# FNet and H3 layers on one core: the order of the queues from a timeline model, with one landing buffer and one work buffer fewer

## The chip, the core and the metric

The kernel runs on one core of one Trainium2 chip. A core has five engines that each work through a queue of their own: TensorE (matmuls; PE in the profile, with its weight loads shown apart as PEld), VectorE (DVE), ScalarE (ACT), GpSimd (POOL) and SyncE (SP, which here only issues transfers). Transfers between the core's memory SBUF and the main memory are issued by SP or ACT and carried by 16 DMA engines. Matmuls write to eight accumulator banks (PSUM). An engine runs its queue strictly in the listed order: an instruction that waits holds up all behind it.

The metric is the time of one execution on the device in microseconds (us). Each kernel was run three times, and one further execution was recorded by the hardware profiler; all durations, waits and clocks come from that record.

## What is computed

Two kinds of layer in turn, twice, on an input of 2048 rows and 576 columns:

```python
def _A_ref(x, dft_seq_re, dft_seq_im, dft_hid_re, dft_hid_im):
    a = jnp.einsum("bsd,ed->bse", x, dft_hid_re)
    b = jnp.einsum("bsd,ed->bse", x, dft_hid_im)
    y = jnp.einsum("ts,bse->bte", dft_seq_re, a) - jnp.einsum("ts,bse->bte", dft_seq_im, b)
    return y

def _B_ref(q, k, v, shift_k, ssm_k, ssm_D):
    ...            # kv = (short causal convolution of k, 4 taps) * v
    ...            # y = causal convolution of kv with ssm_k, length 2048, by FFT
    y = y + kv * ssm_D[None, None, :]
    return q * y

x = A_x
x = x + _A_ref(_layernorm(x), ...)
x = x + _B_ref(_layernorm(x), B_k, B_v, ...)
x = x + _A_ref(_layernorm(x), ...)
x = x + _B_ref(_layernorm(x), B_k, B_v, ...)
```

`_B_ref`'s convolution depends on k, v and the filters alone, and both B layers use the same ones, so its result `y` is computed once. In the kernel this is "the branch". What remains of a B layer is the product of the normed x with `y`.

## The kernel before

Every float32 factor is split into a high and a low part of fewer bits (`split`, line 61: ScalarE copies the high part on line 62, VectorE subtracts on line 63), and each product is three matmuls: high by high, high by low, low by high. All matmuls go through `mm`, so all have line 56 in the profile; they are told apart by what they write.

**Main work, `layer` (line 195).** One FNet layer is 128 steps: 4 row blocks `tb`, each with the real and the imaginary DFT matrix (`g` = 0 and 1), each over 16 chunks `k` of the sequence. A step loads one 128x512 chunk of the matrix (`load_c`: tiles `craw`, three buffers, and its split `csp`, three buffers) and multiplies it with the tile `X[k]` in 14 matmuls of 512 columns into the five banks `s0` to `s4`. Counted over both layers there are 256 steps; steps 0 to 127 are the first layer. After the 16 steps of a group, `evac_u` and `evac_r` bring the five banks to the tiles `u` of that `g` (one buffer each).

**`hidden` (line 170).** With the `u` of both `g`, the DFT along the columns is done for the four `j` of the row block: per `j` two pieces of 27 matmuls of 288 columns into one bank `bk` (three banks in all), against the constants `W`. VectorE adds the residual (line 182), which was landed in a `land` tile, into a `work` tile, and `done0` stores it as `xa` (in the first layer), or `done1` gates it and stores the output (in the second). Eight such pieces of 27 follow each row block; `finish(pending, 1)` spreads them over steps, and `finish(pending, 99)` before the last step of the next `g` = 0 group empties the list, since `evac_u` then writes over the `u` that they read.

**The branch (line 230)** runs beside the first layer, in three stages that hand over through main memory:

- f1: for 16 `j` and two sources (`src` 0 is the product of k's convolution and v, on VectorE, lines 278 to 281; `src` 1 is the filter), a split into a `parts` tile (two buffers), 12 matmuls, four evictions (line 295) into `outp` (three buffers) and two stores to `t_d`. Its constants land through `load_fr` (line 77) into `fc`. The chunks of k and the taps use tiles of the tags `w0` to `w8`, which `load_w` needs later for the constants of `hidden`.
- mid: 64 groups; each lands 288 KB of `t_d` in a `land` tile, splits it to `parts`, multiplies (6 matmuls, two banks), multiplies the two spectra on ScalarE and VectorE (lines 327 to 336, two `work` tiles), splits the product to `yf`, multiplies back (3 matmuls, `mid_inverse`, one bank), evicts (line 347) and stores to `v_d`.
- i2: for 16 `j`, lands `v_d` twice and the constants once, splits, 12 matmuls, two evictions (line 383) and a store to `yb`. Each reads all that mid stored.

**The second layer's x.** `get_x1` (line 431) lands `xa` and `yb`, gates (`gated`, line 393, which takes statistics, a power on GpSimd on line 94, and two VectorE operations, lines 398 and 399), stores `xb`, norms it (`normed`, with a second set of statistics and a second power) and writes the split `X[j]` (`to_x`, line 105: ScalarE on line 107, VectorE on lines 109 and 110). For `j` below 12 it is called from step 113 of the first layer on, for the others within the second layer.

**What sets the order.** The program is written out in one order, by the loops at the end of `fnet_h3_kernel`: line 460 to 467 advance the branch by so many pieces per step, up to fixed step numbers (`F1_END`, `W_END`, `MID_END`, `I2_END`). The framework then schedules it: it knows what each instruction reads and writes, places instructions on their engines' queues with the written order as the priority, holds an instruction back while its data or a free buffer of its tag is missing, chooses the addresses (`auto_bufs=True`) and puts in the semaphores. How many tiles of a tag may be alive at a time is the `bufs=` of the tile: `LAND` for all landings of `land` (x, xa, xb, yb, f1's sources, constants, mid's and i2's inputs, the residuals of `hidden`), `WORK` for `work` (normed and gated x, the residual sums, the convolution of k, mid's products).

Of the kernel before, what the change touches and what calls it, by code (L numbers as in the profile page):

```python
# [34 lines left out]
PREP = 113  # L35
MID_LAG = 2
FC = 3
LAND = 5
WORK = 4
PARTS = 2  # L40
OUTP = 3
CRAW = 3
# [4 lines left out]
def fnet_h3_kernel(ctx: ExitStack, tc: tile.TileContext, x, c_mat, w_re, w_im, k_pad, v, shift_k,  # L47
# [17 lines left out]
    def land(shape=(P, D)):  # L65
        return sb.tile(list(shape), F32, tag="land", bufs=LAND, name="land")

    def work(shape=(P, D)):
        return sb.tile(list(shape), F32, tag="work", bufs=WORK, name="work")

# [481 lines left out]
```

## Time and profile before

| | |
|---|---|
| median of three runs | 1257.85 us (1254.85 to 1259.23) |
| span of the profiled execution, first to last instruction | 1256.2 us |
| mean granted TensorE clock | 0.995 of full speed |
| transfers | 200.46 MB, 160 GB/s over the span |
| busy: VectorE, ScalarE | 724.7 us, 579.5 us |

The profiled execution lies 1.65 us below the median of the runs. Busy times are sums over an engine's instructions; the shares are of the span. They are means over stages that differ: in the first 200 us the DMA engines are busy for 0.83 of the time at 274 GB/s and VectorE for 167 of 200 us, from 750 us on (the second layer without the branch) the same figures are 0.32, 99 GB/s and 164 of 450 us. A row of a group of instructions ends in the idle time that its engine had just before them and in what ended that idle time.

### The profile page before, as it was taken

The page shows a single profiled execution, that of the slowest core. Times are in us where ns is not written, and L with a number is a line of the kernel's source. Part 1 is how long each engine was busy: PE and PEld are TensorE (multiplying, and loading weights), DVE is VectorE, ACT ScalarE, POOL GpSimd, SP SyncE. Part 2 cuts the span into 40 slices and gives each one's busy share as a digit, 9 for nine tenths or more (in the row PEclk, how much of TensorE's full clock was granted, in tenths as well). Part 3 has the DMA queues.
Part 4 walks back from the last instruction along what each step waited for, and adds up shares of the span by engine and source line. Part 5 has one row for each costly group of instructions (what it writes and reads, how often), then busy time and mean ns, then how long its engine had stood idle before and what let it go on. Part 6 is the DMA issues. An engine that isn't in the chain of part 4 may idle for free.

```text
span 1256.2 us, 17885 instructions
## 1 busy us (share of the span) xinstructions
PE 1221.6 (97%) x6464; PEld 1059.2 (84%) x6464; DVE 724.7 (58%) x1404; ACT 579.5 (46%) x1166; POOL 54.5 (4%) x68
## 2 busy tenths in 40 slices
PE   7999999999999999999999899999999999999997
PEld 6778788898889888889887898889888988898887
DVE  7799893858865698853488846243324323333324
ACT  6865565758855698853663414221222113201320
POOL 1100000000000000000012201000000000000001
PEclk9999999999999999999999999999999999999999
DMA  8879876745543455447886545223322422233201
GB/s 301 298 249 302 259 256 225 231 124 166 156 135 120 144 159 171 131 153 265 267 280 214 175 141 172 81 87 100 104 84 69 125 88 77 83 100 115 84 35 58
DMA packets 113131, 200.46 MB, mean 160 GB/s; under 512 B 11665, under 2 KB 36241, under 8 KB 113042
## 3 DMA queue, kind: packets, MB, share of 16 engines
q1 hardware_dynamic: 84114, 166.27, 42.6%
q10 hardware_dynamic: 28928, 33.04, 7.4%
q8 instruction: 51, 0.84, 0.3%
q14 instruction: 38, 0.31, 0.1%
HBM read 152.08 MB, written 47.19 MB: 159 GB/s over the span
## 4 chain that ended last, share of the span: by engine, by line
PE 76%; DMA 9%; DVE 6%; ACT 5%; issue 2%; POOL 1%; SPq 0%; ACTq 0%; POOLq 0%; DVEq 0%
PE s L56 50%; PE bk L56 26%; DMA t<-outp 5%; DMA craw<-in_c_mat 2%; POOL rs L94 1%; DVE bst L88 1%; ACT csp L62 1%; DMA land<-t 1%; ACT outp L295 1%; DVE work L399 1%; DVE x L110 1%; DVE parts L63 0%; DVE csp L63 0%; DVE u L63 0%; DMA land<-vd 0%
## 5 line engine op out<-in xcount | busy, mean ns | idle before, releaser
L56 PE MATMUL s<-csp,x 128*128 128x512 f32 x3584 | 855.7, 391 | 3.4 <-DVE csp L63 2.5
L56 PEld LDWEIGHTS s<-csp,x 128*128 128x128 f32 x3584 | 664.1, 188 | 134.2 <-DVE csp L63 3.4
L62 ACT ACTIVATE csp<-craw 128x512 fp32r<-128x512 f32 x256 | 160.6, 629 | 444.3 <-PE s L56 440.5
L63 DVE TENSOR_TENSOR csp<-craw,csp 128x512 fp32r<-128x512 f32 x256 | 176.3, 689 | 313.9 <-ACT csp L62 312.7
L56 PE MATMUL bk<-w,u 128*128 128x288 f32 x1536 | 217.2, 297 | 3.9 <-DVE u L63 2.7
L56 PEld LDWEIGHTS bk<-w,u 128*128 128x128 f32 x1536 | 210.6, 189 | 9.0 <-DVE u L63 3.1
L56 PE MATMUL bk<-parts,fc 128*128 128x288 f32 x576 | 94.8, 306 | 15.8 <-ACT parts L62 8.1
L56 PEld LDWEIGHTS bk<-parts,fc 128*128 128x128 f32 x576 | 86.4, 193 | 26.3 <-ACT outp L295 11.1
L63 DVE TENSOR_TENSOR parts<-land,parts 128x576 fp32r<-128x576 f32 x112 | 84.7, 757 | 29.2 <-ACT parts L62 25.3
L94 POOL TENSOR_TENSOR rs<-ve,mhalf 128x1 f32<-128x1 f32 x56 | 47.6, 851 | 1161.9 <-DVE ve L92 1129.7
L62 ACT ACTIVATE parts<-land 128x576 fp32r<-128x576 f32 x112 | 76.4, 683 | 13.9 <-DMA land<-vd 7.1
L182 DVE TENSOR_TENSOR work<-land,bk 128x288 f32<-128x288 f32 x64 | 28.8, 452 | 88.1 <-PE bk L56 86.3
L56 PE MATMUL bk<-parts,mc 128*128 128x288 f32 x384 | 67.2, 300 | 1.6 <-ACT parts L62 1.0
L295 ACT ACTIVATE outp<-bk 128x288 f32<-128x288 f32 x128 | 47.6, 405 | 41.6 <-DMA t<-outp 28.4
L56 PEld LDWEIGHTS bk<-parts,mc 128*128 128x128 f32 x384 | 56.7, 189 | 8.1 <-ACT parts L62 2.5
L62 ACT ACTIVATE u<-s 128x512 fp32r<-128x512 f32 x64 | 36.4, 599 | 28.1 <-PE bk L56 17.8
L278 DVE TENSOR_TENSOR work<-kr,wt 128x576 f32<-128x576 f32 x64 | 47.1, 752 | 1.7 <-DMA kr<-in_k_pad 1.4
L63 DVE TENSOR_TENSOR u<-s,u 128x512 fp32r<-128x512 f32 x64 | 42.5, 687 | 7.0 <-ACT u L62 6.9
L56 PE MATMUL bk<-yf,mc 128*128 128x288 f32 x192 | 39.7, 303 | 2.3 <-ACT outp L347 1.7
L56 PEld LDWEIGHTS bk<-yf,mc 128*128 128x128 f32 x192 | 32.4, 189 | 10.6 <-ACT outp L347 2.6
L334 DVE TENSOR_TENSOR work<-bk,work 64x288 f32<-64x288 f32 x64 | 29.4, 459 | 19.1 <-ACT work L330 18.6
L62 ACT ACTIVATE yf<-work 128x288 fp32r<-128x288 f32 x64 | 28.3, 442 | 22.8 <-DVE work L336 20.4
(56 smaller groups left out, 702.6 us busy)
## 6 DMA issues: line engine op xcount, KB each, us to landing
craw<-in_c_mat SPq DMA_DIRECT2D x256, 256.0 KB, 3.1
t<-outp ACTq DMA_DIRECT2D x64, 288.0 KB, 4.3
land<-t SPq DMA_DIRECT2D x64, 288.0 KB, 3.0
land<-in_x SPq DMA_DIRECT2D x32, 288.0 KB, 3.6
vd<-outp ACTq DMA_DIRECT2D x64, 144.0 KB, 3.1
land<-vd SPq DMA_DIRECT2D x32, 288.0 KB, 4.3
land<-yb SPq DMA_DIRECT2D x32, 288.0 KB, 3.1
kr<-in_k_pad SPq DMA_DIRECT2D x10, 576.0 KB, 6.2
```

The lines of the kernel that those rows point to most:

```text
L56: nc.tensor.matmul(ps, lhsT, rhs, start=first, stop=last)
L62: nc.scalar.activation(h, src, AF.Copy)
L63: nc.vector.tensor_tensor(l, src, h.bitcast(F32), OP.subtract)
L88: nc.vector.bn_stats(st[:, i, :], src[:, i * HD:(i + 1) * HD])
L94: nc.gpsimd.tensor_tensor(rs, ve, mhalf, OP.pow)
L110: nc.vector.tensor_tensor(t[:, D + REM:], y[:, :NC * P], h[:, :NC * P], OP.subtract)
L182: nc.vector.tensor_tensor(xa[:, cs], r[:, cs], ps[:, :HD], OP.add)
L278: nc.vector.tensor_tensor(tmp if t else r, kr[j + t], w, OP.mult)
L295: nc.scalar.activation(so[:, c, :], ps[:, :HD], AF.Copy)
L334: nc.vector.tensor_tensor(p2[lo], px[hi, :HD], kk[hi, 1, :], OP.mult)
L399: nc.vector.scalar_tensor_tensor(q, q, rs, xa, op0=OP.mult, op1=OP.add)
```

## The change

`LAND` goes from 5 to 4, `WORK` from 4 to 3, and the framework's scheduler is told to run its timeline model of the machine while it places the instructions: an instruction goes onto its queue at the moment at which the model has its engine free and its inputs and buffers there. Instructions, sizes and the written order stay.

```diff
-LAND = 5
-WORK = 4
+LAND = 4
+WORK = 3
...
-    with tile.TileContext(nc, auto_bufs=True) as tc:
+    with tile.TileContext(nc, auto_bufs=True, schedule_with_timeline_sim=True) as tc:
         fnet_h3_kernel(tc, **args, out=o)
```

## The prediction

> **What bounds the kernel now.** I read the page first (busy shares), then the chain of waits, then the windows by stage for the two kinds of matmul, then the groups by form and the DMA issues, and last the order in which the built kernels list their instructions on each engine.
>
> ```profile
> PE 1221.6 (97%) x6464; PEld 1059.2 (84%) x6464; DVE 724.7 (58%) x1404; ACT 579.5 (46%) x1166; POOL 54.5 (4%) x68
> ```
>
> TensorE is busy 97% of the span, so what is left to win is small. How small, the chain says: in its undisturbed stretches it gives the pace of both matmuls.
>
> ```profile
> 746.83 3.60 PE bk L56 x27
> 750.43 79.36 PE s L56 x350
> ```
>
> 350 matmuls of 512 columns (`s`) in 79.36 us are 0.2267 us each; 27 of 288 columns (`bk`) in 3.60 (the next in 3.55) are 0.1324 each. All 3584 `s` and 2880 `bk` make 812.5 + 381.3 = 1193.8 us. No order can go below that; the span has 62 us more. Where they lie, the windows tell (columns: width; busy and count of these matmuls; granted clock; DMA share; GB/s). First `s`, then `bk`:
>
> ```profile
> 0.00:200.00 200.00, 139.79 (x564) 0.99 0.83 274
> ...
> 650.00:750.00 100.00, 66.24 (x283) 0.98 0.57 185
> 750.00:1200.00 450.00, 367.77 (x1604) 1.00 0.32 99
> ```
>
> ```profile
> 0.00:200.00 200.00, 60.37 (x348) 0.99 0.83 274
> ...
> 650.00:750.00 100.00, 31.45 (x215) 0.98 0.57 185
> 750.00:1200.00 450.00, 90.18 (x652) 1.00 0.32 99
> ```
>
> Width minus counts times paces: 0 to 200 loses 200 - 564 x 0.2267 - 348 x 0.1324 = 26 us, 750 to 1200 loses 0.1, and 650 to 750 (the change of layers) 7.4. By the same sum 200 to 250 loses 3.5, 250 to 500 12, 500 to 650 5, and the end after 1200 6.5. So the second layer can only get worse, and before it some 50 us are lost, 6.6 of them before the first matmul.
>
> **What the change does to the order.** All instructions and their sizes stay; what moves is their place. I counted them in the listed orders. "Step" is one of the 256 C chunks (14 `s` matmuls, 3.17 us).
>
> 1. The branch falls behind. When step 32 is done, 240 of 384 f1 matmuls are listed in the kernel before, 159 in the changed one; by step 48, 384 against 282. By step 96, 360 mid matmuls against 264. By step 112, 156 i2 matmuls against none.
> 2. Three things wait for the branch. The w tiles share tags with `kr` and `wt`, so `load_w` follows f1; `hidden` needs w; `evac_u` at the end of each g = 0 group needs the u tiles that `hidden` reads. So steps 48 and 112 can't go on until f1, respectively the last mid groups and 216 `hidden` matmuls, are through. `get_x1` needs all of i2.
> 3. So three stretches have no `s` work for cover: after step 47, 87 f1 matmuls in a row and then 39 mid and inverse ones; after step 111, seven mid groups; and in steps 128 to 138 each step is listed directly behind the x it needs. Before step 128 the kernel before has 9 of the second layer's 16 x written, the changed one 1.
>
> **What each costs.** The rows:
>
> ```profile
> L295 ACT ACTIVATE outp<-bk 128x288 f32<-128x288 f32 x128 | 47.6, 405 | 41.6 <-DMA t<-outp 28.4 <-PE bk L56 12.1 <-ACT outp L295 0.3
> ...
> L328 ACT ACTIVATE work<-bk 64x288 f32<-64x288 f32 x64 | 25.8, 403 | 0.9
> ```
>
> ```profile
> t<-outp ACTq DMA_DIRECT2D x64, 288.0 KB, 4.3
> land<-t SPq DMA_DIRECT2D x64, 288.0 KB, 3.0
> ...
> vd<-outp ACTq DMA_DIRECT2D x64, 144.0 KB, 3.1
> land<-vd SPq DMA_DIRECT2D x32, 288.0 KB, 4.3
> ```
>
> **A, up to step 47.** Fewer f1 items run here, and 0 to 200 moves 274 GB/s at a DMA share of 0.83, so some of its 26 us should come back. 15.6 of them lie in the first 50 us (132 `s`, 34 `bk`), where x and C must land either way; the other 11 could. Against it, SP now issues 4.6 MB of `kr` and `wt` among the first five x loads (8.7 MB up to the fifth, 3.3 before); 5.4 MB at the 300 GB/s of the page's first slice delay it by 18 us, of which the first steps' own matmuls hide part: a loss up to 12. I take 0, near the middle of -11 and +12. POOL's list is the same as before.
>
> **B, step 47 to 48.** f1: 86 matmuls are 11.4 us. ScalarE needs 29 x 0.405 (L295) + 7 x 0.683 (parts) + 1.3 (fc, mc) = 17.8; the 16 stores and five loads, 5.8 MB, need 19 us at 300 GB/s and 23 at 250. I take 20.5: 9 us of stall (6.5 to 11.5). Then the first mid load must follow the last store: 0.4 + 4.3 + 3.0 + 0.68 (split) less 0.8 of matmuls still to run = 7.6 (5 to 9). SP queues the w loads behind that load, so they are late too. Up to the first `hidden` VectorE has 6 x 0.757 (parts) + 10 x 0.755 (w) + 20 x 0.455 (L333 to L336) + 4 x 0.456 (yf) = 23.0 us, ScalarE 21.2, TensorE 64 x 0.132 = 8.5: 14.5, of which I take 13 (11 to 18), since some loads land during the wait before. Less the 3.5 lost there now: **+26** (19 to 35).
>
> **C, steps 48 to 79.** Mid groups are spread thinner among the steps, so some of the 12 us comes back: **-4** (-8 to +3). Around step 80, six mid groups between `hidden` pieces of 27 (3.57 us each, against 3.1 of ScalarE per group): **+2** (0 to 6).
>
> **D, step 111 to 112.** One mid group is 4 x 0.403 + 0.683 + 0.442 + 0.410 = 3.15 us of ScalarE, and the next group's bank comes free only behind L335. Seven groups are 22 us at the least (28 if evictions and VectorE follow each other, 4.0 each); I take 3.5 each, 24.5, against 8.5 us of matmuls: +16 (13.5 to 19.5). What stands behind the waits there: in ScalarE's queue L347 waits for the inverse matmul, and behind it are the next group's L327 to L330, for which L333 and the next bank wait. Then i2: last eviction 0.4, store 3.1, load 4.3, split 0.68, less 1.1 of cover: +7.4 (6 to 9). The alternating i2 and `hidden` pieces after it, four landings in flight instead of five: +4 (0 to 10). Less today's 5: **+22** (15 to 34).
>
> **E, steps 128 to 143.** One x costs VectorE 0.86 + 0.20 + 0.15 (statistics), 0.81 + 0.82 (L398, L399), 0.91 + 0.20 + 0.15, 0.21, 0.22 + 0.68 (L109, L110) = 5.2 us, with the step's csp 0.69 5.9, against 3.17 of TensorE. The two POOL powers (0.85 each, one pair per x) stand between VectorE instructions that need them; 7.2 with their wait whole. I take 6.5. Ten x: 65 + 3.2 for the last step, against 35.4 of matmuls listed there: +33 (27 to 40). The 135 `hidden` matmuls then cover the next x's; the last four follow too closely (chain from `hidden` to x some 16 us by rows: 0.46, store 2.3, load 3.1, then the x): +6 (0 to 10). Less today's 7.4: **+32** (20 to 43).
>
> **F, the clock.** Long gaps cost twice:
>
> ```profile
> 45.00:50.00 5.00, 1.93 (x11) 0.94 0.83 306
> 50.00:55.00 5.00, 5.00 (x18) 0.72 0.73 244
> ```
>
> 3.1 us idle, and the next 5 us run 18 matmuls at 0.72 where 24 fit at 1.00: 6 x 0.227 = 1.4 us. Four long gaps (two in B, two in D): **+6** (0 to 12). In E a slower matmul hides behind VectorE. The Trainium skill, "TensorE: Matmul & The Clock Gate", section "What's actually happening", says the array's clock falls to half after an idle window of about 3.4 us and is freed after about as long a busy one; the dip after the 3.1 us above agrees. By that rule the sparse mid stretches run at half clock too, and F would be nearer 12.
>
> The end (6.5) and steps 144 to 255 stay: there every matmul's producer is listed over 3 us of matmul work ahead, as before.
>
> **Sum:** 0 + 26 - 4 + 2 + 22 + 32 + 6 = +84 on the profiled 1256.2: 1340. The runs' median is 1.65 above that span, so 1342.
>
> **Rivals.**
> - *Thinner stalls, one price:* each clump takes only what its busiest engine is busy, and A gives its 11 back: the low ends, -11 + 19 - 8 + 0 + 15 + 20 + 0 = +35, 1293. For it: engine rows are hard minima, waits are my reading. Against: one queue feeds the next in turn. Chance 0.17 (up to 1310).
> - *The first stages become free of DMA (not slower):* if the loss up to step 111 is all DMA pressure, thinning the branch gives back 26 - 6.6 + 3.5 + 12 = 35 us, and the clumps' engines run far enough ahead for B and D to add nothing; it decides where E stays under 35: 1258 - 35 + 32 = 1255. For it: the 0.83 share and 28.4 us of waits on stores in L295's row. Against: `parts` has two buffers, so splits can't run ahead by more than two items, and mid needs banks, three in all. Chance 0.04.
> - *Half clock:* the clump matmuls and each restart at half pace, plus the high ends of B, D and E: +110 to +140, 1368 to 1398. For it: the dip shown. Against: in the clumps TensorE isn't the bound. Chance 0.17.
> - *It does nothing:* two fewer buffers and the same order. Excluded by the listed orders, which differ in over half their rows.
>
> The forecast itself, between 1310 and 1368, has 0.62. The low and high ends added up give 1293 and 1403 (+145); the range 1296 to 1390 leaves out about 0.1 on either side. A measurement here tells some 0.3% (4 us) from no change. The second rival's 0.04 is halved between faster and same, as its 1255 lies at the border: faster 0.02, same 0.02, slower 0.96.
>
> **What would show it.** TensorE's busy share falls to about 92%. Its waits go to L295 and parts at step 48 (around 210 to 260 us), to L330, L335, L347 and then parts at step 112 (around 570 to 620), and to x (L107, L109, L110) in steps 128 to 143. By the windows some 30 us are lost at each of the three, and nothing after the last. Wrong would be: less than 10 us lost at step 48 (then B's engines ran ahead), or steps 128 to 138 at 3.2 us each (then the x were ready, and E falls).

## The result, and the profile after

The changed kernel takes 1353.64 us (median, 1351.17 to 1354.97) against 1256.35 us of the kernel before (1254.64 to 1259.23), each over four executions with the profiled one among them: the ratio is 1.0765 (95% interval 1.0742 to 1.0789). It is slower, by 97 us where 84 were forecast and inside the range. The profiled execution has a span of 1349.4 us, 93.2 above the span before, and a mean clock of 0.962. A few executions in the experiments took far longer than all others of their kernel (1497.77 us at a clock of 0.754 is one) and are left out of times and ratios; the one that was profiled of the kernel with the two buffers alone is of that kind, so of that kernel only the time is used.

The busy line of the page: TensorE has the same 6464 matmuls, which now fill 93% of a longer span.

```profile
PE 1253.0 (93%) x6464; PEld 1083.2 (80%) x6464; DVE 730.8 (54%) x1404; ACT 588.9 (44%) x1166; POOL 44.1 (3%) x68
```

The waits of TensorE in the changed kernel (total us, times, longest):

```profile
PE s L56 <- ACT x L107: 31.6, 16, 3.2
PE bk L56 <- ACT parts L62: 26.9, 5, 8.6
PE bk L56 <- ACT yf L62: 13.9, 9, 3.1
PE bk L56 <- ACT outp L295: 9.2, 7, 3.7
PE bk L56 <- ACT work L330: 4.3, 5, 1.1
```

The first row is the second layer's x (20.1 us, from 750 us on) and the first layer's own x at the start (11.5 us, in the first 100); `parts` is the start of each stage, `yf` and L330 are mid groups without cover, L295 is f1's.

Where they lie, the windows tell, first for `s`, then for `bk` (width; busy and count; granted clock; DMA share; GB/s). Before:

```profile
0.00:100.00 100.00, 72.92 (x294) 0.98 0.85 284
550.00:650.00 100.00, 54.06 (x224) 1.00 0.78 260
```

```profile
0.00:100.00 100.00, 20.45 (x100) 0.98 0.85 284
550.00:650.00 100.00, 50.66 (x357) 1.00 0.78 260
```

After:

```profile
0.00:100.00 100.00, 62.02 (x239) 0.91 0.69 227
...
200.00:300.00 100.00, 26.69 (x106) 0.83 0.63 205
...
600.00:750.00 150.00, 59.45 (x242) 0.92 0.59 191
750.00:900.00 150.00, 96.03 (x359) 0.93 0.55 170
```

```profile
0.00:100.00 100.00, 11.06 (x51) 0.91 0.69 227
...
200.00:300.00 100.00, 57.08 (x309) 0.83 0.63 205
...
600.00:750.00 150.00, 81.43 (x491) 0.92 0.59 191
750.00:900.00 150.00, 35.46 (x256) 0.93 0.55 170
```

Width minus counts times the two full paces (0.2267 and 0.1324) is the time lost in a stretch: in the first row after 100 - 239 x 0.2267 - 51 x 0.1324 = 39.1. The table has this sum for the matching stretches of both kernels, and the prediction's terms (half of F, the clock, put to B and half to D). The stretches do not hold the same steps, since the branch lags: 550 us is in step 99 before, 600 us in step 109 after.

| stretch (us before; after) | lost before | lost after | moved | predicted |
|---|---|---|---|---|
| start (0-100; 0-100) | 20.1 | 39.1 | +19.0 | A: 0 for both rows |
| (100-200; 100-200) | 5.8 | 0.4 | -5.4 | |
| around step 48 (200-250; 200-300) | 3.5 | 35.1 | +31.6 | B and F: +29 |
| between (250-550; 300-600) | 14.3 | 6.8 | -7.5 | C and step 80: -2 |
| around step 112 (550-650; 600-750) | 2.0 | 30.1 | +28.1 | D and F: +25 |
| change of layers (650-750; 750-900) | 7.4 | 34.7 | +27.3 | E: +32 |

The moves add up to 93.1 of the span's 93.2. After 900 us nothing is lost (0.5 in 400), as forecast. Four terms are within 6 us, and their misses cancel in part (+2.6 and +3.1 against -5.5 and -4.7). The start is not: nothing was predicted there, and 13.6 us came, about as much as the whole forecast is off.

### The profile page after: what moved, and what is told of

Same layout as the page of the kernel before. It is cut to its first block, busy times and chain, and to the rows that moved or that the text cites. A ratio compares the mean times of both kernels' runs of the same rounds, so it can differ in the third digit from the quotient of the medians.

```text
span 1349.4 us, 17915 instructions
## 1 busy us (share of the span) xinstructions
PE 1253.0 (93%) x6464; PEld 1083.2 (80%) x6464; DVE 730.8 (54%) x1404; ACT 588.9 (44%) x1166; POOL 44.1 (3%) x68
## 4 chain that ended last, share of the span: by engine, by line
PE 81%; ACT 5%; DVE 4%; DMA 3%; issue 2%; POOL 0%; ACTq 0%; SPq 0%; POOLq 0%; DVEq 0%
PE s L56 55%; PE bk L56 26%; DMA t<-outp 1%; DVE bst L88 1%; ACT x L107 1%; ACT outp L295 1%; ACT csp L62 0%; DVE work L399 0%; ACT parts L62 0%; DVE work L398 0%; ACT work L330 0%; ACT work L102 0%; DVE x L110 0%; ACT work L329 0%; DMA land<-in_x 0%
## 5 line engine op out<-in xcount | busy, mean ns | idle before, releaser
L56 PE MATMUL s<-csp,x 128*128 128x512 f32 x3584 | 882.0, 396 | 32.2 <-ACT x L107 31.6
L56 PE MATMUL bk<-w,u 128*128 128x288 f32 x1536 | 222.0, 299 | 1.5 <-ACT work L330 1.2
L56 PE MATMUL bk<-parts,fc 128*128 128x288 f32 x576 | 101.4, 311 | 28.5 <-ACT parts L62 19.0
L56 PEld LDWEIGHTS bk<-parts,fc 128*128 128x128 f32 x576 | 92.1, 200 | 39.4 <-ACT parts L62 20.5
L56 PE MATMUL bk<-parts,mc 128*128 128x288 f32 x384 | 79.2, 325 | 13.6 <-ACT parts L62 7.9
L56 PEld LDWEIGHTS bk<-parts,mc 128*128 128x128 f32 x384 | 67.3, 208 | 24.2 <-ACT parts L62 8.5
L182 DVE TENSOR_TENSOR work<-land,bk 128x288 f32<-128x288 f32 x64 | 28.7, 452 | 97.1 <-PE bk L56 92.4
L94 POOL TENSOR_TENSOR rs<-ve,mhalf 128x1 f32<-128x1 f32 x56 | 38.7, 700 | 1264.8 <-ACT outp L383 671.6
L295 ACT ACTIVATE outp<-bk 128x288 f32<-128x288 f32 x128 | 49.7, 408 | 53.0 <-PE bk L56 43.4
L333 DVE TENSOR_TENSOR work<-bk,work 128x288 f32<-128x288 f32 x64 | 29.2, 457 | 59.8 <-ACT work L328 33.1
L56 PE MATMUL bk<-yf,mc 128*128 128x288 f32 x192 | 46.9, 319 | 13.9 <-ACT yf L62 13.9
L56 PEld LDWEIGHTS bk<-yf,mc 128*128 128x128 f32 x192 | 36.0, 203 | 20.8 <-ACT yf L62 16.8
L62 ACT ACTIVATE yf<-work 128x288 fp32r<-128x288 f32 x64 | 28.4, 443 | 29.3 <-DVE work L336 28.7
```

The source lines that it names most:

```text
L56: nc.tensor.matmul(ps, lhsT, rhs, start=first, stop=last)
L62: nc.scalar.activation(h, src, AF.Copy)
L94: nc.gpsimd.tensor_tensor(rs, ve, mhalf, OP.pow)
L182: nc.vector.tensor_tensor(xa[:, cs], r[:, cs], ps[:, :HD], OP.add)
L295: nc.scalar.activation(so[:, c, :], ps[:, :HD], AF.Copy)
L333: nc.vector.tensor_tensor(p1, px[:, :HD], kk[:, 0, :], OP.mult)
```

## The experiments

All are read against the kernel before on the same chip (1255 to 1257 us in the medians); ratios carry their 95% interval. "Lost" is the sum just shown.

### The two buffers alone

```diff
-LAND = 5
-WORK = 4
+LAND = 4
+WORK = 3
```

> The kernel before with LAND 4 and WORK 3 alone, scheduled as before. Theory (the new order costs the time; the two buffers only matter through it): 1250 to 1264 us, within 0.6% of before, and no long wait at steps 47, 111 or 128. Rival (one landing and one work buffer fewer starve the branch, which then lags): 1285 us or more, with waits for land or work tiles in f1 and mid.

1265.70 us, ratio 1.0078 (1.0052 to 1.0104): +10 us, 2 more than my theory allowed and far from the rival. I then took the landing buffer alone (`LAND = 4`):

> The kernel before with LAND 4 alone, WORK 4 and the schedule as before. LAND 4 with WORK 3 had cost 9.8 us. Theory (the landing buffer costs it: SP's queue waits for a buffer, with the loads of C and x behind it, in the first 100 us): 1261 to 1266, the loss in the first 100 us. Rival (the work buffer costs it, through normed x and the convolution of k): within 3 us of before.

1264.4 us, ratio 1.0063 (1.0040 to 1.0086): +8, so most of the 10 is the landing buffer's, and the intervals leave it open whether the work buffer costs anything. 24.0 us are lost in its first 100 us against 20.1: 3.9 of the 5.3 us by which its span is above the one before. No other stretch moves by more than 1 us (6.6 against 5.8 in the second 100, 20.7 against 19.8 from 200 to 650, 8.3 against 7.4 at the change of layers). The other way (`LAND = 6`):

> The kernel before with LAND 6, all else as it was. LAND 4 cost 7.9 us. Theory (SP's queue still waits for landing buffers with five, with C and x behind it): 1249 to 1254, some us won in the first 100. Rival (five are enough, or a sixth only moves bytes to a busier moment): 1254 to 1259.

1259.32 us, ratio 1.0028 (1.0015 to 1.0042): 3.5 us slower, at the upper end of the rival's range. The theory falls: five are enough in the old schedule.

### k's chunks among the first x

In the listed order of the changed kernel SP issues k's chunks and the taps early: in its trace eight of these transfers (576 KB each) go out ahead of the fifth x, where the kernel before has none. By hand in the kernel before, at the head of f1:

```diff
+        load_w4()
+        for i in range(6):
+            load_k(i)
+        loaded[0] = 6
         todo = [(j, 1) for j in range(K_FIRST)] + [(j, 0) for j in range(K_FIRST)]
```

> The kernel before with k's chunks for all the branch's early items and the taps landed among the first x loads instead of one by one ahead of the item that needs them. Theory (those 4.6 MB delay the first x and constants; this is the loss of the changed kernel's first 100 us): +10 to +20 us, 1267 to 1277, the loss within the first 100 us. Rival (the first 100 us are lost to how the landings of x are ordered against each other with four buffers, not to k): under +5, at most 1262.

1264.29 us, ratio 1.0063 (1.0041 to 1.0085): +8, between the two theories. 26.5 us are lost in the first 100 us, 6.4 more than before, so the place is right and the size was too high. But the hand-made order is only half a copy: in its trace four of the eight transfers go out ahead of the fifth x and the others up to 40 us, so 6.4 is not the whole price that they have in the changed kernel. With both buffers cut as well:

> LAND 4, WORK 3 and k's early chunks and taps landed among the first x loads, otherwise the order before. Theory (the changed kernel's loss in its first 100 us is these two parts together, 10 and 9 us): 1270 to 1279, with the loss in the first 100 us. Rival (both are the same waiting of SP's queue and overlap): 1264 to 1269.

1271.94 us, ratio 1.0119 (1.0092 to 1.0146): the time is nearly the sum of the parts, but its first 100 us lose 27.7, 7.6 more than before, where the landing buffer (3.9) and k (6.4) alone add up to 10.3. So the time lies in the theory's range, and in the start the two overlap, as the rival had it. The copy is weaker still here: two of the eight transfers go out ahead of the fifth x.

### f1's last quarter without cover

LAND 4 and WORK 3, f1 thinned over the first 45 steps, and the rest of it and the loads of w behind step 46:

```diff
+        if n == 46:
+            want = 32
+        elif n < 46:
+            want = K_FIRST + 22 * n // 46
...
-        if F1_END < n <= W_END:
-            for _ in range(-(-9 // (W_END - F1_END))):
+        if n == 46:
+            for _ in range(9):
```

> The order before, LAND 4 and WORK 3, with f1 thinned so that its last quarter, the loads of w and nothing of mid stand between steps 46 and 48. To be read against the kernel with these buffers alone. Theory (f1's evictions, stores and loads set the pace of a clump without cover): f1's clump takes 18 to 22 us against 10 of matmuls, +15 to +25 us in all, less what thinning gives back earlier (up to 5). Rival (the engines run ahead of the clump and it goes at matmul pace): under +5.

1287.83 us, ratio 1.0248 (1.0225 to 1.0271) to the kernel before and 1.0248 / 1.0078 = 1.017, or +21 us, to the buffers alone. Around step 48 (200 to 300 us) 18.3 us are lost against 3.9. The clump's last 75 matmuls, 9.9 us of work, go from 227.36 to 249.68 in the timeline, 12.4 us more. Meanwhile ScalarE's evictions (L295) wait 8.0 us for stores to free their tile, and TensorE waits for the evictions. So f1's evictions and stores set its pace; the rival falls. But the clump is only 12.4 of the 21, so that the time lies in the theory's range is in part luck. What I had not expected: the first 100 us lose 32.0, though the second give back 3.8. This pacing puts seven items into the first 16 steps where the kernel before has four, so f1 competes with the first x, as I read it.

### The last mid groups without cover

The buffers as before; mid's groups spread to step 110, the rest of them behind it, and i2 in the eight steps that follow:

```diff
-        elif n <= MID_END:
-            want = 32 + 64 * (n - F1_END) // (MID_END - F1_END)
+        elif n < 110:
+            want = 32 + 53 * (n - F1_END) // 70
+        elif n == 110:
+            want = 96
         else:
-            want = min(113, 96 + 17 * (n - MID_END) // (I2_END - MID_END))
+            want = min(113, 96 + 17 * (n - 110) // 8)
...
-        if n > W_END:
+        if W_END < n < 96 or n > 110:
```

> The order and buffers before, with mid thinned so that nine mid groups stand in a row behind step 111, hidden's 189 matmuls behind them, and i2 after those in eight steps. Theory (ScalarE sets the pace of a mid group without cover, 3.5 to 3.8 us against 1.2 of matmuls): 18 to 24 us in the clump, 3 to 6 more at the change of layers, since x follows i2 (5 of 16 x written by then): +20 to +30, 1275 to 1286. Rival (mid's engines run ahead through the three banks): under +6.

1278.53 us, ratio 1.0181 (1.0135 to 1.0226): +23, in the theory's range. The timeline shows the groups at an even pace (start; length; idle time before and its releaser):

```profile
591.29 0.61 PE L56 MATMUL bk<-yf,mc 128*128 128x288 f32 x1 [1.01 <-ACT yf L62]
...
595.02 0.61 PE L56 MATMUL bk<-yf,mc 128*128 128x288 f32 x1 [1.01 <-ACT yf L62]
```

3.73 us per group, of which 9 x 0.1324 = 1.2 are matmuls, and each waits for `yf`. That ScalarE sets this pace is only part of it. Two groups in a row, each from one inverse matmul to the next (width; busy and count of TensorE, its weight loads, VectorE, ScalarE, GpSimd; clock; DMA share; GB/s):

```profile
576.92:580.12 3.20, 1.99 (x10) 1.31 (x10) 2.90 (x7) 2.94 (x8) 0.00 (x0) 0.98 0.58 179
580.12:583.84 3.72, 2.71 (x9) 2.22 (x10) 2.95 (x7) 2.92 (x8) 0.00 (x0) 0.50 0.46 130
```

ScalarE and VectorE do the same work in both. At full clock ScalarE is busy for nearly the whole group; at half clock a group takes 0.5 us longer, and ScalarE's eviction L347 waits 0.7 us for the inverse matmul instead of 0.2. TensorE is a link of the chain there, though it is far from busy with matmuls of full pace.

### The second layer's x, late

`PREP = 200` in the kernel before: `get_x1` is called in the second layer alone.

> The kernel before with the second layer's x written inside that layer alone (1 of 16 is written before step 128, as in the changed kernel; 9 before). Theory (the x chain sets the pace of steps 128 to 138): each of those steps waits 2 to 3 us for x and takes 5 to 6 us, +20 to +30 us, 1278 to 1288. Rival (x written on time is hidden behind the matmuls, and the loss after step 128 in the changed kernel comes from elsewhere, such as i2 being late): under +6, at most 1263.

1271.14 us, ratio 1.0112 (1.0088 to 1.0137): +14, half of what I expected. The steps without cover have the expected pace:

```profile
772.92 3.53 PE L56 MATMUL s<-csp,x 128*128 128x512 f32 x14 [1.29 <-ACT x L107]
778.62 3.72 PE L56 MATMUL s<-csp,x 128*128 128x512 f32 x14 [2.17 <-ACT x L107]
```

That is 5.7 us from step to step (5.9 to the next one). But there are fewer such steps: in this kernel's list hidden's last matmuls stand between steps 128 and 135, 13 to 27 to a step, and cover the wait. In the changed kernel 135 of them stand in a row behind step 138. So I held them back, calling `finish` in the second layer only from step 136 on:

```diff
-        finish(pending, 1)
+        if n == 8:
+            finish(pending, 99)
+        elif n > 8:
+            finish(pending, 1)
```

> The kernel with the second layer's x in that layer alone (1271 us), and in it hidden's pieces held back in the written order until step 136, so that 81 of those 216 matmuls stand behind step 138. Theory (in the changed kernel the late x cost 27 us and not 14 because hidden's matmuls were spent elsewhere than between the steps that wait for x): 81 x 0.132 = 10.7 us less cover, +5 to +11 on the kernel with late x, 1276 to 1283. Rival (the position of hidden's matmuls does not matter, since x is late by the same amount): 1268 to 1274.

1277.85 us, ratio 1.0171 (1.0148 to 1.0193): +7 on the kernel with late x alone, and the time lost at the change of layers (650 to 800 us) goes from 21.7 to 28.5. That is 21 more than the 7.4 before, against 27.3 in the changed kernel. The rival falls: the same late x costs more where its cover stands behind it.

### All parts together

k's early chunks, LAND 4 and WORK 3, f1's and mid's clumps and the late x in one kernel with the old schedule:

> All four parts of the changed order built by hand into the old schedule, with LAND 4 and WORK 3: k's early chunks among the first x, f1's last quarter behind step 46, the last mid groups behind step 111, the second layer's x in that layer alone. Theory (the parts make the difference and add): 1255 + 18 + 21 + 23 + 14 = 1331, with 1318 to 1350. Rival (the loss is in the fine order of the timeline schedule, which this kernel does not copy): under 1305.

1335.72 us, ratio 1.0635 (1.0607 to 1.0664): +80 of the changed kernel's +97, with the expected sum missed by 5. The first 100 us lose 34.7 (39.1 in the changed kernel), and 600 to 900, both late stretches, 61.8 (64.8). Around step 48 it is 18.6 against 35.1; there this kernel has f1's clump, but not the 39 mid and inverse matmuls behind it. So in the two late stretches the lag of the branch and of x, written by hand, costs about what it costs under the timeline model. The start agrees by another way: thinning f1 by hand loses 32.0 us there even without k's chunks, and puts 93 of the branch's matmuls ahead of step 16, where the changed kernel has 51.

### The timeline order with the old buffers

```diff
-CRAW = 3
-CSP = 3
+CRAW = 2
+CSP = 2
```

and LAND 5, WORK 4 in the changed kernel.

> The changed kernel's timeline schedule with LAND 5 and WORK 4 as before; so that this fits, CRAW and CSP go from 3 to 2. Theory (the timeline order makes the loss; the two buffers about 10 us of it): 1335 to 1365, with the same three losses at steps 48, 112 and 128. Rival (the buffers starve the branch under the timeline): under 1300.

1333.16 us, ratio 1.0619 (1.0590 to 1.0648), 2 us below the theory's range. The order makes most of the loss: 29.7 us are lost around step 48, 27.3 around 112, 30.0 at the change of layers. Giving the buffers back takes away 20 us, not 10, and half of it, 39.1 - 28.7 = 10.4, in the first 100 us. (CRAW and CSP are smaller here, so 20 is the net of both edits.)

SP's waits in the first 100 us, for the landing buffer of the next x (line 419), which is free once ScalarE has normed an earlier one (lines 411 and 102). First the changed kernel, then this one:

```profile
SPq L419 <- ACT work L411: 13.8, 3, 7.1
SPq L419 <- ACT work L102: 12.3, 6, 5.7
```

```profile
SPq L419 <- ACT work L102: 5.4, 3, 3.8
...
SPq L419 <- ACT work L411: 3.5, 3, 1.7
```

26.1 us against 8.9. In all SP waits about as long in both (72.4 and 69.2 us, all rows summed); in the second it waits for C's buffers instead (28.5 us on line 125, against 1.9). While SP waits for a place for x, nothing behind it is issued, the next chunks of C among it: from 50 to 100 us the changed kernel moves 175 GB/s at a DMA share of 0.57, this one 226 at 0.72.

### One more eviction buffer

`OUTP = 4` in the kernel before, since f1's evictions are what TensorE waits for there:

> The kernel before with OUTP 4 in place of 3, all else as it was. TensorE waits 7.7 us for f1's evictions (L295) there, and those wait for stores to free their buffer. Theory (a fourth buffer takes part of that away): 1248 to 1253. Rival (stores of f1 are held up by the DMA engines in the first 200 us, and another buffer only moves the wait): 1254 to 1259.

1254.95 us, ratio 0.9996 (0.9984 to 1.0009): the same time, as the rival had it. None of the kernels beats the one before.

## Why the prediction held, and which term failed

**A, the start: the term that was mis-sized.** The prediction took 0, between -11 and +12. Measured: +19.0 in the first 100 us, -5.4 in the second, +13.6 together. Cut by steps, its two parts stand apart. Steps 16 to 47 lose 1.5 us (96.8 to 232.8 us) against 11.2 (76.8 to 268.6), so the gain from the thinned f1 came nearly in full. All before step 16 loses 39.0 us against 18.2: 20.8 more, where the delay of the first steps was priced at 12 at most. The fifth x goes out at 22.5 us, in the kernel before at 10.4. The working had counted the bytes that k puts ahead of x, but gave the buffer that is missing there no price: it named four landings in flight only in D.

What the runs put in its place, in the first 100 us: the timeline order with the old buffers loses 28.7, that is +8.6, and the step to four and three buffers under it +10.4 more (net, since CRAW and CSP were smaller in the first). In the old order one landing buffer is +3.9, k's early chunks, half copied, +6.4. How the +8.6 splits between k's bytes and the order of x on SP, and the +10.4 between LAND and WORK, stays open: no run changes one of these alone.

**B, step 48: right** (+29 with its clock, +31.6 measured). Lines of the changed kernel's timeline:

```profile
234.15 1.75 PE L56 MATMUL bk<-parts,fc 128*128 128x288 f32 x12
...
240.91 5.83 PE L56 MATMUL bk<-parts,fc 128*128 128x288 f32 x24 [3.71 <-ACT outp L295]
...
261.73 2.12 PE L56 MATMUL bk<-parts,mc 128*128 128x288 f32 x6 [5.79 <-ACT parts L62]
...
283.52 4.93 PE L56 MATMUL bk<-w,u 128*128 128x288 f32 x24 [0.68 <-ACT work L330]
```

f1's clump took from 234.15 to the idle time before 261.73, that is to 255.94: 21.8 us (20.5 predicted); the start of mid waited 5.79 (7.6); mid and w took 283.52 - 261.73 = 21.8 (8.5 + 14.5 = 23, of which 21.5 were entered). VectorE is busy for 19.6 us of these and ScalarE for 19.3, so the bound was the one named. The working set 64 matmuls against it, where its own list and the trace have 39 (5.2 us): the stall was 16.6, with 13 entered.

**C: right in sign.** -7.5 against -2, inside its bounds.

**D, step 112: right** (+25 with its clock, +28.1 measured).

```profile
624.61 0.61 PE L56 MATMUL bk<-yf,mc 128*128 128x288 f32 x1 [1.02 <-ACT yf L62]
...
628.40 0.61 PE L56 MATMUL bk<-yf,mc 128*128 128x288 f32 x1 [1.02 <-ACT yf L62]
...
635.54 4.73 PE L56 MATMUL bk<-w,u 128*128 128x288 f32 x24 [0.55 <-ACT work L330]
...
662.50 3.48 PE L56 MATMUL bk<-parts,fc 128*128 128x288 f32 x12 [4.91 <-ACT parts L62]
```

A group takes 3.79 us (3.5 predicted), and its wait is for `yf`, which the prediction did not name. The clock is 0.50 from 620.81 to 632.21 us, and the kernel with mid's last groups without cover shows what that does: 3.20 us a group at full clock, 3.72 at half. So the prediction's 3.5 came near with one link of the chain left out. The start of i2 waited 4.91 (7.4).

**E, steps 128 to 143: right in mechanism, 5 us too high** (+32, +27.3 measured). An x was priced at 6.5 us; it takes 5.7 to 5.8:

```profile
788.29 5.08 PE L56 MATMUL s<-csp,x 128*128 128x512 f32 x14 [2.30 <-ACT x L107]
...
799.90 3.47 PE L56 MATMUL s<-csp,x 128*128 128x512 f32 x14 [2.29 <-ACT x L107]
```

The window over five such steps of the changed kernel (width; busy and count of TensorE, its weight loads, VectorE, ScalarE, GpSimd; clock; DMA share; GB/s):

```profile
788.29:816.98 28.69, 20.50 (x70) 15.05 (x70) 25.05 (x71) 10.69 (x15) 5.32 (x10) 0.88 0.70 210
```

28.69 / 5 = 5.74 us per step, with VectorE busy for 25.05 of 28.69: it sets the pace. The 5.9 us of listed VectorE work were no lower bound, though: VectorE is busy for 5.01 per step with the same 14 instructions. Their durations add up to more, since in the trace one starts some 0.08 us before the one ahead of it ends: the two statistics L88 of one tile, 0.45 and 0.44 us, take 0.81 together at 794.86. That leaves 0.73 per step, of which 0.62 is the wait of L100 for GpSimd's power (3.1 us in five steps). The listed order has the gate of one x and the norm of the one before side by side, so there is one such wait per x.

**F, the clock: right at the restarts, too little between them.** Behind the long gaps 24 matmuls of `hidden` took 4.93 and 4.73 us, against 3.37 for 24 later ones: 1.4 to 1.6 us each, where 1.4 was predicted. But in the sparse mid stretches the clock stayed at half (0.50 from 261.73 to 283.52 and from 620.81 to 632.21 us), which the prediction considered. Its sum left that out, on the ground that TensorE is not the bound there. It is part of the chain: by the 0.5 us a group above, some 2.5 us for five groups in D, an estimate.

**The rivals.** "Thinner stalls, one price" falls with B and D, which came out at or above the forecast. "The first stages become free of DMA" is wrong at both ends: the DMA share did fall (0.85 to 0.69 in the first 100 us), and the loss there doubled; 10.4 of the rise of 19.0 go with the two buffers. "Half clock" is seen in the restarts and in the mid groups, but costs a few us as far as these lines show it, and not what that rival asked. That the change does nothing was excluded by the lists, and by the ratio.

## What to carry to other kernels

A schedule that places what is ready first uses up the long run of independent matmuls early and leaves the slow chain without cover. Before pricing it, count in the listed order how far each side branch is when the main work comes to the point that needs it; each piece left there costs the pace of the chain that makes it (here 3.2 to 3.8 us for a mid group with 1.2 us of matmuls), not that of TensorE. Take an engine's share in such a chain from its busy time in a window: the durations of the rows added up were 0.9 us too long per x here. A buffer taken from a tag that many loads share is priced at the start of the kernel too, where an in-order queue that waits for it holds up every load behind it.

## What the runs showed of the hardware

In steps 128 to 138 the same 14 matmuls took 5.0 to 5.1 us in some steps and 3.5 in the others, though TensorE had waited 2.3 us ahead of both kinds (the two lines under E). The trace's clock record has half speed for 3.41 us each from 788.62, 805.69 and 822.76 us. These are 17.07 us apart, that is 5 x 3.41, while a step takes some 5.8. The Trainium skill, "TensorE: Matmul & The Clock Gate", section "What's actually happening", calls the clock's window free-running and some 3.4 us long; the trace agrees with both. Cut into such stretches, it also shows what decides (width; busy and count of TensorE; clock; DMA share; GB/s):

```profile
785.21:788.62 3.41, 1.11 (x5) 1.00 0.59 173
788.62:792.04 3.42, 3.42 (x10) 0.50 0.89 263
795.45:798.86 3.41, 2.15 (x10) 1.00 0.89 248
798.86:802.28 3.42, 2.38 (x10) 1.00 0.63 206
```

The wait ahead of 788.29 lies within one stretch, which leaves TensorE busy for 1.11 us of it, and the next stretch runs at half clock. The wait ahead of 799.90 is shared by two stretches, busy for 2.15 and 2.38, and the clock stays. So a wait of 2.3 us is enough or not, by where it falls; where the border lies between 1.1 and 2.1 us of work, these steps do not show. The slow steps cost nothing here: steps start 5.5 to 5.8 us apart, slow or not, since each waits for x.
